# Two transformer-like layers on one core: part of the sum over phi(K) moves from TensorE to GpSimd and VectorE, with new instruction orders

## The chip, the core and the metric

One NeuronCore of a Trainium2 chip runs the whole program in one launch. The metric is the device time of one execution in microseconds (us), as the median of several runs. The engines are TensorE (PE in the profile, its weight loads PEld), VectorE (DVE), ScalarE (ACT), GpSimd (POOL) and SyncE (SP), which only issues transfers here.

## The reference

Input x has 2048 rows (tokens) of 512 values, in bf16. Two blocks A and B alternate twice (A, B, A, B), each added to x, with the layer norm in front applied twice in block B. Cut to what matters:

```python
def _A_ref(x, wqkv, wo):                       # 32 heads of 16
    q, k, v = heads(x @ wqkv)
    phi = lambda t: jnp.where(t > 0, t + 1, jnp.exp(t)) + 1e-6
    pq, pk = phi(q), phi(k)
    kv = jnp.einsum("bhsd,bhse->bhde", pk, v)
    z = jnp.einsum("bhsd->bhd", pk)            # the sum over all tokens
    num = jnp.einsum("bhqd,bhde->bhqe", pq, kv)
    den = jnp.einsum("bhqd,bhd->bhq", pq, z)[..., None] + 1e-6
    return (num / den) merged @ wo

def _B_ref(x, w1, b1, w2, b2):                 # 512 -> 1792 -> 512
    y = _layernorm(x)
    return gelu(y @ w1 + b1) @ w2 + b2

x = x + _A_ref(_layernorm(x), wqkv, wo)
x = x + _B_ref(_layernorm(x), w1, b1, w2, b2)
# and both once more
```

The change is about z in the first block A.

## The kernel before

The 2048 tokens are 16 tiles of 128, in 4 chunks of 4 tiles. "Layer one" is the first A and B (index 0 in names), "layer two" the second (index 1). The program builds a graph of some 1550 operations and plays them in an order that is written out by hand for each engine (`ORDER`), with fixed buffer places (`PLACES`) and, for steps that several engines can do, a fixed engine (`WAY`). Each engine works strictly through its own list; an operation whose input is not there holds up all that stand behind it. Names carry layer, chunk or tile, and part. SyncE issues the transfers, among them the transposing DMAs, also in a written order.

The steps, by the names used below (tile t, chunk c, layer L, part k):

- Norm of a tile: `statsA` and `aggrA` (L775, L777, VectorE), `vepsA` (L782) and `powA` (L784, GpSimd), then `normA` on VectorE (L803) or, with `nmrA` before it (L795, GpSimd), on ScalarE (L798). The norms of block B have the same names with B. `TA` and `TB` are the transposing DMAs of the result (L812, SyncE); the first tiles are transposed on TensorE instead (`PTC`, `PTA`, L825).
- `K L_t` (L879) and `Q L_c_k` (L896, L909): projections, each 4 matmuls of 128x512. phi is `exp` and `relu` on ScalarE (L847, L858), `min` (L860, L851) on VectorE, and `phik` or `phiq` (L864 as a sum, on VectorE or GpSimd; L853 as a maximum that reads PSUM, on VectorE). phi(K) of a tile lies in one of 10 buffers `pkb`.
- `G L_t_0` (L984 in layer one, L1013 in layer two): the products of normed x and phi(K), 4 matmuls a tile in layer one.
- z: `Z L_c` (L970) multiplies the four phi(K) tiles of a chunk by a column of ones, 16 matmuls with one column each, and `zs L_c` (L941, L944, VectorE) adds the four columns to `zs`. Layer one does so for all four chunks. Layer two does it for the last chunk only: the first three are added up in fp32 in `zacc` by `za` (L958, VectorE or GpSimd); then `zhi` (L923) and `zlo` (L926) split the sum into two bf16 parts and `ZH` (L933, L934), 8 matmuls with one column, gives z, which `zsh` takes over.
- From zs, `zb` (L1040) and `dz` (L1045) are made on VectorE. zb is the weight of `D 0_0_k` (L1100); dz gives `ZR` (L1048) and a row of z (L997). `KV`, `kvm` and `M` (L1034, L1053, L1057) fold wv, the G sums and wo into one weight `gtb`; its copies to SBUF are `cpg`, `cpz`, `cpm` (L997, L1000).
- The denominators of chunk 0: `D`, then `ln` and `rec` on ScalarE (L1102, L1104) and `pr` (L1108). Of the others, token by token: `pz` (L1077), `red` (L1080), `den`, `rec` (L1083, L1085), `pr` (L1089), and a transposing DMA `TP` (L1093).
- `WO` (L1123) and `RA` (L1128) close block A. Block B: `W1 L_c_f_h` with the chunk c (L1153; halves of 256 columns in chunk 0, h being the half), `gelu` (L1158), `b2` (L1139: x plus b2, VectorE or GpSimd), `W2 L_t_0` and `W2 L_t_7` (L1190, 7 matmuls each) and `RB` (L1196, L1200). `OD` stores the result. In names such as `W10_1_13_0` the first digit after W1 is the layer; `W20_0_7` is the second half of W2 of tile 0 in layer one.
- `warm` (L749) are matmuls on constants at the start. `wv`, `wo`, `w1`, `w2` are weight loads that GpSimd issues, `b1z` clears a buffer for `b1`, which SyncE loads and transposes (`Tb1`).

The order of TensorE around the change, layer one (parts left out):

```
... PTA0_2 K0_1 PTA0_3 K0_2 K0_3 G0_0_0 G0_1_0 Q0_0_2 Q0_0_1 Q0_0_0 K0_5 G0_2_0 K0_4 Z0_0 G0_3_0 ...
... K0_12 Z0_1 K0_15 K0_10 K0_8 K0_9 K0_11 G0_7_0 Q0_1_1 Z0_3 Q0_0_3 Z0_2 G0_8_0 G0_9_0 D0_0_2 ...
```

Of the kernel before, what the change touches and what calls it, by code (L numbers as in the profile page):

```python
# [1359 lines left out]
```

## Time and profile before

| | us |
|---|---|
| median of 3 runs | 323.65 (322.83 to 324.69) |
| the profiled execution | 323.1 |
| its span, first to last instruction | 321.9 |
| TensorE busy | 318.0 |
| VectorE busy | 218.1 |
| ScalarE busy | 189.3 |
| GpSimd busy | 145.5 |

The granted TensorE clock is 1.00 throughout. A line such as L958 is a line of this kernel's source. Several operations of one kind share a line, so a group of a line mixes layers; single instructions are found by their start in the span. A matmul's duration in the profile includes its way through the array (0.38 us for 128x512), while the chain that ended last gives the time from one to the next (0.86 us for four). "Waits" list how long an engine stood idle before an instruction, and which instruction ended the wait.

### The profile page before, as it was taken

How to read it: one execution, taken by the hardware profiler on the slowest of the kernel's cores; microseconds unless marked ns; L12 is line 12 of the kernel's file. 1: busy time of each engine (PE TensorE's matmuls, PEld its weight loads, DVE VectorE, ACT ScalarE, POOL GpSimd, SP SyncE). 2: the span in 40 equal slices, each digit the busy share in tenths (PEclk: the TensorE clock that was granted, in tenths of full speed). 3: DMA queues.
4: the chain of work that ended last, by engine and by line, in shares of the span. 5: the costliest groups of instructions: out<-in, count | busy, mean ns of one | idle time of the engine just before them, and what ended most of it. 6: DMA issues, size and time to landing. Idle time of an engine off the chain costs nothing.

```text
span 321.9 us, 4748 instructions
## 1 busy us (share of the span) xinstructions
PE 318.0 (99%) x1703; PEld 157.4 (49%) x1703; DVE 218.1 (68%) x529; ACT 189.3 (59%) x324; POOL 145.5 (45%) x216
## 2 busy tenths in 40 slices
PE   8999999999999999999999999999999999999997
PEld 3444554666444444444444444558544444444444
DVE  5998789999786774028848899999889881101103
ACT  5898656797730636667962367979634442663320
POOL 6573978688655355101822415887454163000000
DMA  7844793142121412111010200122232322201002
GB/s 257 200 81 85 241 348 85 35 82 36 33 49 34 82 33 51 34 33 32 18 40 10 51 16 0 35 51 52 50 62 54 98 65 67 49 0 35 16 33 65
DMA packets 52355, 21.68 MB, mean 67 GB/s; under 512 B 47532, under 2 KB 50860, under 8 KB 52332
## 3 DMA queue, kind: packets, MB, share of 16 engines
q1 hardware_dynamic: 50844, 16.37, 22.4%
q0 software_dynamic: 1056, 4.72, 4.3%
q10 hardware_dynamic: 432, 0.30, 0.3%
q8 instruction: 13, 0.21, 0.3%
q14 instruction: 10, 0.08, 0.1%
HBM read 8.00 MB, written 2.10 MB: 31 GB/s over the span
## 4 chain that ended last, share of the span: by engine, by line
PE 97%; DMA 2%; DVE 0%; issue 0%
PE ps L1153 30%; PE ps L1190 29%; PE ps L1123 9%; PE ps L879 8%; PE ps L896 6%; PE ps L984 4%; PE ps L1013 4%; DMA t<-in_A_x_dram 2%; PE ps L909 2%; PE ps L1176 1%; PE ps L970 1%; PE ps L1034 1%; PE ps L1057 1%; PE ps L1100 1%; DVE stats L775 0%; PE ps L1048 0%
## 5 line engine op out<-in xcount | busy, mean ns | idle before, releaser
L1158 ACT ACTIVATE gT<-ps,b1c 128x512 bf16<-128x512 f32 (+1 forms) x140 | 77.0, 601 | 68.7 <-PE ps L1153 68.1
L1153 PE MATMUL ps<-t,w 128*128 128x512 bf16 (+1 forms) x560 | 102.5, 336 | 0.0
L1190 PE MATMUL ps<-w,gT 128*128 128x512 bf16 x434 | 98.6, 379 | 0.0
L1153 PEld LDWEIGHTS ps<-t,w 128*128 128x128 bf16 x560 | 54.8, 98 | 43.7 <-ACT gT L1158 0.2
L1190 PEld LDWEIGHTS ps<-w,gT 128*128 128x128 bf16 x434 | 42.5, 98 | 50.4
L784 POOL TENSOR_TENSOR rstd<-veps,neghalf 128x1 f32<-128x1 f32 x64 | 39.0, 625 | 41.1 <-DVE veps L782 38.9
L847 ACT ACTIVATE eb<-ps 128x512 bf16<-128x512 f32 x62 | 35.4, 606 | 19.3 <-PE ps L896 7.3
L1200 DVE TENSOR_TENSOR yb<-ps,xsb 128x512 bf16<-128x512 f32 x15 | 10.2, 688 | 41.4 <-PE ps L1190 41.4
L775 DVE BATCH_NORM_STATS2 stats<-xsb 128x6 f32<-128x512 f32 x48 | 32.0, 681 | 0.3
L1123 PE MATMUL ps<-gtb,t 128*128 128x512 bf16 x128 | 31.4, 379 | 0.0
L879 PE MATMUL ps<-wqkv,t 128*128 128x512 bf16 x128 | 30.9, 379 | 0.3 <-ACT t L835 0.3
L858 ACT ACTIVATE rb<-ps 128x512 bf16<-128x512 f32 x43 | 25.3, 607 | 5.8 <-PE ps L879 5.8
L798 ACT ACTIVATE yb<-xsb,nmr,rstd 128x512 bf16<-128x512 f32 x21 | 16.9, 814 | 15.1 <-POOL nmr L795 15.1
L896 PE MATMUL ps<-wqkv,t 128*128 128x512 bf16 x96 | 24.1, 379 | 0.0
L1089 POOL TENSOR_TENSOR t<-t,rr 128x512 bf16<-128x512 bf16 x18 | 19.3, 1072 | 9.0 <-DVE rr L1085 6.4
L782 POOL TENSOR_SCALAR veps<-mv 128x1 f32<-128x1 f32 x35 | 8.2, 236 | 32.7 <-DVE mv L777 31.3
L1196 DVE TENSOR_TENSOR xsb<-ps,xsb 128x512 f32<-128x512 f32 x16 | 10.8, 678 | 17.9 <-PE ps L1190 17.9
L1139 POOL TENSOR_TENSOR xsb<-xsb,b2b 128x512 f32<-128x512 f32 x17 | 21.4, 1267 | 3.0 <-DVE yb L803 2.9
L1077 POOL TENSOR_TENSOR lr<-t,zrow 128x512 f32<-128x512 bf16 x14 | 16.5, 1179 | 7.3 <-ACT zrow L997 4.5
L1123 PEld LDWEIGHTS ps<-gtb,t 128*128 128x128 bf16 x128 | 12.5, 98 | 14.5
L803 DVE TENSOR_SCALAR yb<-xsb,mv,rstd 128x512 bf16<-128x512 f32 x27 | 14.5, 542 | 7.3 <-POOL rstd L784 6.0
L879 PEld LDWEIGHTS ps<-wqkv,t 128*128 128x128 bf16 x128 | 12.1, 98 | 14.7 <-ACT t L835 0.9
(99 smaller groups left out, 363.7 us busy)
## 6 DMA issues: line engine op xcount, KB each, us to landing
w<-in_B_w_dram POOLq DMA_DIRECT2D x4, 896.0 KB, 9.1
out_dram<-yb SPq DMA_DIRECT2D x15, 128.0 KB, 2.0
t<-in_A_x_dram SPq DMA_DIRECT2D x3, 512.0 KB, 4.8
t<-yb SPq DMA_TRANSPOSE x62, 2.5
wqkv<-in_A_wqkv_dram SPq DMA_DIRECT2D x1, 512.0 KB, 5.9
wqkv<-in_A_wqkv_dram POOLq DMA_DIRECT2D x1, 512.0 KB, 4.7
wo<-in_A_wo_dram POOLq DMA_DIRECT2D x1, 512.0 KB, 5.3
t<-in_A_x_dram SPq DMA_DIRECT2D x1, 384.0 KB, 3.3
```

Source lines behind the costliest of these rows:

```text
L775: G.op("dve", lambda e: e.bn_stats(stats[:, s.slot, :], src()), 620, reads=src_keys, writes=[k + "s"], tiles=[s, *src_tiles], name=f"stats ...
L784: G.op("pool", lambda e: e.tensor_tensor(rstd[:, s.slot:s.slot + 1], veps[:, s.slot:s.slot + 1], neghalf[:], op=ALU.pow), 570, reads=[k + ...
L847: G.op("act", lambda e: e.activation(eb[:, et.slot, :], bank(bt), ACT.Exp, scale=by()), 478, reads=[src_key, *more_keys], writes=[f"e{tag} ...
L858: G.op("act", lambda e: e.activation(rb[:, rt.slot, :], bank(bt), ACT.Relu, scale=by()), 478, reads=[src_key, *more_keys], writes=[f"r{tag ...
L879: ins = e.matmul(bank(b), lhsT=yTa(yT)[:, dt, k * P:(k + 1) * P], rhs=wqkv[:, dt, D:2 * D], start=(i == 0 and n == 0), stop=(i == len(part ...
L896: ins = e.matmul(bank(b), lhsT=yTa(yT)[:, dt, k * P:(k + 1) * P], rhs=wqkv[:, dt, 0:D], start=(dt == 0), stop=(dt == DT - 1))
L1089: lambda e, d=d, tok=tok, heads=heads: e.tensor_tensor(heads(tok()), heads(tok()), rr[:, d.slot, :].unsqueeze(2).broadcast_to([P, H, DH]), ...
L1123: ins = e.matmul(bank(wb), lhsT=yTa(pq)[:, kt, k * P:(k + 1) * P], rhs=gtb[:, kt, :], start=(kt == 0), stop=(kt == DT - 1))
L1139: G.op("pool" if on_pool else "dve", lambda e: e.tensor_tensor(xsb[:, st, :], xsb[:, st, :], b2b[:], op=ALU.add), 1120 if on_pool else 600 ...
L1153: ins = e.matmul(bank(b, n), lhsT=w1[:, dt, ft * P:(ft + 1) * P], rhs=yTa(yT)[:, dt, k0 * P:k1 * P], start=(dt == 0), stop=(dt == DT - 1))
L1158: G.op("act", lambda e, ft=ft, b=b, k0=k0, k1=k1, n=n: e.activation(gT[:, g.slot, ft * 512 + k0 * P:ft * 512 + k1 * P], bank(b, n), ACT.Ge ...
L1190: ins = e.matmul(bank(b), lhsT=gT[:, g.slot, ft * 512 + k * P:ft * 512 + (k + 1) * P], rhs=w2[:, ft, :], start=(ft == 0), stop=(ft == FT - 1))
```

## The change

In layer one, phi(K) of chunks 0 and 1 (8 tiles, 7 additions) is summed in fp32 in `zacc`: zaA1 and zaA3 to zaA7 on GpSimd, zaA2 on VectorE. Z0_0, Z0_1, zs0_0 and zs0_1 go; zhiA and zloA (VectorE), ZHA (TensorE, 8 matmuls with one column) and zshA (VectorE) come. The code for it was in `attn_z` already, and an entry of `WAY` selects it:

```diff
+        "zaA2": "dve", "zc0": "0 1",
```

The orders of all engines and the buffer places are chosen anew. Parts of TensorE's, VectorE's and GpSimd's:

```diff
 TensorE
-K0_5 G0_2_0 K0_4 Z0_0 G0_3_0 ... K0_12 Z0_1 K0_15 K0_10 K0_8 K0_9 K0_11 G0_7_0 Q0_1_1 Z0_3 Q0_0_3 Z0_2 G0_8_0 G0_9_0 D0_0_2
+Q0_1_0 K0_4 G0_2_0 K0_5 G0_3_0 ... K0_14 K0_10 K0_8 K0_11 K0_9 G0_7_0 Q0_0_3 Z0_3 G0_8_0 Z0_2 Q0_1_1 ZHA G0_9_0 D0_0_2
-W20_1_0 W10_0_10_0 W20_0_0 W10_0_9_1 ... W10_0_13_1 W10_0_5_1 W10_1_3_0 W10_1_9_0 W10_1_8_0
+W20_1_0 W20_0_0 W20_0_7 W10_0_4_1 W10_0_12_1 W10_0_5_1 W10_0_13_1 W20_1_7 W10_0_2_1 WO0_9_0 W10_0_7_1 W10_0_9_1 W10_0_8_1 W10_0_6_1 W10_0_0_1 W10_0_10_1 W10_1_13_0
 VectorE
-normA0_2 statsA0_5 normA0_3
+normA0_2 normA0_1 statsA0_4 normA0_3
-phik0_9 phik0_11 zs0_2 zs0_3 zb0 minq0_0_3 minq0_1_1 dz0
+mink0_10 zhiA phik0_10 mink0_9 mink0_11 phik0_9 phik0_11 zloA zs0_2 zs0_3 zshA zb0 dz0
-normB0_5 normB0_4 pz0_2_0
+pr0_2_1 normB0_5 RB0_0 minq0_3_0 red0_2_3 b20_1 statsA1_0 normB0_4
-cpm1_0 rec1_1_0 phiq1_1_3 rec1_1_1 RA1_0
+cpm1_0 pr1_0_2 pr1_1_0 rec1_1_1 phiq1_1_3 RA1_0
 GpSimd
-nmrA0_15 b1z nmrA0_8 powA0_12 vepsA0_10 powA0_10 vepsA0_11 powA0_11 nmrA0_10 vepsA0_9 powA0_9 nmrA0_11 phik0_14 eps6 wv wo phik0_8 w1_0
+nmrA0_15 zaA3 powA0_12 zaA4 vepsA0_10 powA0_10 nmrA0_10 vepsA0_8 zaA5 powA0_8 nmrA0_8 vepsA0_9 vepsA0_11 powA0_11 nmrA0_11 powA0_9 zaA6 zaA7 phik0_14 phik0_8 b1z wv wo w1_0
```

Other steps change engine in `WAY`: from GpSimd to VectorE 14 `b2` adds, 8 `pr`, 4 `pz`, 2 `za` and 12 of the small `veps`; from VectorE to GpSimd 2 `b2`, 3 `pr`, 3 `pz`, 1 `za` and 9 `veps`. The warm-up matmuls at the start keep their number and sizes; five of the 256 wide stand ahead of the first transpose instead of three. TensorE's order from `W11_3_11_0` on, late in layer two, is nearly the same. The code also gains a list of the order of chunks (`CHUNKS`, here 0 to 3 as before) and a way of treating half a chunk (`by_half`), which no entry of `WAY` uses.

More of the change, by code (lines that the diff above doesn't have):

```diff
@@ L887, in attn_q, with fn @@
         def attn_q(L, c, yT, pq):
-            if by_token(L, c):
-                for k in range(4):
+            half = by_half(L, c)
+            own = pq
+            if half:
+                own = tokq[(L, c)] = Tile(T4, f"pqt{L}_{c}")
+            n = 2 * P if half else 4 * P
+            if not by_token(L, c):
+                for kt in range(DT):
+                    b = Tile(psum, f"q{L}_{c}_{kt}" + "c" * half, "q")
+                    def fn(e, kt=kt, b=b):
+                        for dt in range(DT):
+                            ins = e.matmul(bank(b, n), lhsT=wqkv[:, dt, kt * P:(kt + 1) * P], rhs=yTa(yT)[:, dt, 0:n],
+                                           start=(dt == 0), stop=(dt == DT - 1))
+                        return ins
+                    G.op("pe", fn, 4 * MM if n == D else 4 * (n / 2.4 + 2.5), reads=[f"yT{L}_{4 * c + k}" for k in range(n // P)] + ["wq"], writes=[f"q{L}_{c}_{kt}" + "c" * half],
+                         tiles=[b, yT], name=f"Q{L}_{c}_{kt}" + "c" * half, lat=MM_DRAIN, n=4)
+                    phi(b, f"q{L}_{c}_{kt}" + "c" * half, lambda kt=kt: yTa(pq)[:, kt, 0:n], f"pq{L}_{c}_{kt}" + "c" * half, [pq], f"q{L}_{c}_{kt}" + "c" * half, n=n)
+            for k in range(4):
+                if by_token(L, c, k):
                     b = Tile(psum, f"q{L}_{c}_{k}", "q")
@@ L900, in attn_q, with attn_z @@
                          tiles=[b, yT], name=f"Q{L}_{c}_{k}", lat=MM_DRAIN, n=4)
[L901 removed]
+                    phi(b, f"q{L}_{c}_{k}", lambda k=k: t4[:, own.slot, k * D:(k + 1) * D], f"pq{L}_{c}_{k}", [own],
                         f"q{L}_{c}_{k}")
[L903 to L914 removed]
         zfirst = {}
[L918 to L920 removed]
+        def attn_z(L, c, pks, order):
+            by_sum = [int(v) for v in (eng("zc0") or "").split()] if L == 0 else order[:NC - 1]
+            others = [v for v in order if v not in by_sum]
             def fold(add):
@@ L973, in attn_z, with attn_g_held @@
             G.op("pe", fn, 400, reads=[f"pk{L}_{4 * c + k}" for k in range(4)] + ["onesm"], writes=[f"zc{L}_{c}"], tiles=[b, *pks], name=f"Z{L}_{c}", lat=MM_DRAIN, n=16)
-            total(b, f"zc{L}_{c}", f"zs{L}_{c}", bool(L) or c != min(v for v in range(NC) if v not in by_sum))
-            if L == 0 and by_sum and c == max(v for v in range(NC) if v not in by_sum):
+            total(b, f"zc{L}_{c}", f"zs{L}_{c}", bool(L) or c != others[0])
+            if L == 0 and by_sum and c == others[-1]:
                 fold(True)
-        def attn_g_held(L, st, k, y, ykey, pk, gb):
-            parts = [(dc,) for dc in range(DT)] if st == ST - 1 else [tuple(range(DT))]
+        def attn_g_held(L, st, k, y, ykey, pk, gb, first, last):
+            parts = [(dc,) for dc in range(DT)] if last else [tuple(range(DT))]
             for part in parts:
@@ L1004, in attn_g_out, with attn_g_chunk @@
                 copy(gtb[:, dc, :], gb, f"g{L}_{dc}", ("gt", dc), dc % 2, f"g{L}_{dc}", off=dc)
-        def attn_g_chunk(L, c, ys, ykeys, pks):
+        def attn_g_chunk(L, c, ys, ykeys, pks, first, last):
             for dc in range(DT):
@@ L1042, in attn_kv @@
                  reads=["zs", "bdmask"], writes=["zb"], name=f"zb{L}", lat=40, fast=True)
-            if any(by_token(L, c) for c in range(NC)):
+            if any(by_token(L, c, 3) for c in range(NC)):
                 zr = Tile(psum, f"zr{L}", "t")
@@ new lines, in attn_den @@
+            half = by_half(L, c)
+            src = tokq[(L, c)] if half else pq
+            pt = pq if half or not by_token(L, c) else Tile(T4, f"pt{L}_{c}")
+            n = 2 * P if half else 4 * P
+            if not by_token(L, c):
+                for kt in range(DT):
+                    tag = f"{L}_{c}_{kt}" + "c" * half
+                    b = Tile(psum, f"d{tag}", "n")
+                    r = Tile(LR, f"lr{tag}")
+                    key = f"pq{L}_{c}_{kt}" + "c" * half
+                    G.op("pe", lambda e, kt=kt, b=b: e.matmul(bank(b, n), lhsT=zb[:, kt * P:(kt + 1) * P], rhs=yTa(pq)[:, kt, 0:n], start=True, stop=True),
+                         MM if n == D else n / 2.4 + 2.5, reads=[key, "zb"], writes=[f"d{tag}"], tiles=[b, pq], name=f"D{tag}", lat=MM_DRAIN)
+                    G.op("act", lambda e, b=b, r=r: e.activation(lr[:, r.slot, 0:n], bank(b, n), ACT.Ln, bias=eps6[:]), 575 if n == D else 362,
+                         reads=[f"d{tag}", "eps6"], writes=[f"l{tag}"], tiles=[b, r], name=f"ln{tag}", lat=90, table="exp")
+                    G.op("act", lambda e, r=r: e.activation(lr[:, r.slot, 0:n], lr[:, r.slot, 0:n], ACT.Exp, scale=-1.0), 536 if n == D else 323,
+                         reads=[f"l{tag}"], writes=[f"l{tag}"], tiles=[r], name=f"rec{tag}", lat=110, table="exp")
@@ new lines, in attn_den, with attn_out @@
+                     1150 if on_pool else 600, reads=[f"rr{tag}", f"pq{tag}"], writes=[f"pq{tag}"], tiles=[d, src],
+                     name=f"pr{tag}", lat=60, fast=not on_pool)
+                dma("sp", lambda e, k=k, tok=tok: e.dma_start_transpose(yTa(pt)[:, :, k * P:(k + 1) * P], tok()), [f"pt{tag}"],
+                    tiles=[src, pt], reads=[f"pq{tag}"], name=f"TP{tag}", sem=("pT", src, k), transpose=True)
+            return pt
+        def attn_out(L, c, k, pq, base, base_keys, base_tiles, first):
@@ L1116, in attn_out @@
             st = 4 * c + k
             wb = Tile(psum, f"wo{L}_{st}", "w")
-            parts = [(kt,) for kt in range(DT)] if st == 0 else [tuple(range(DT))]
+            parts = [(kt,) for kt in range(DT)] if first else [tuple(range(DT))]
             for part in parts:
@@ L1141, in mlp_front, with mlp_up @@
                  fast=not on_pool)
-        def mlp_up(L, c, yT, g):
-            parts = [(0, 2), (2, 4)] if c == 0 else [(0, 4)]
+        def mlp_up(L, c, yT, g, first):
+            parts = [(0, 2), (2, 4)] if first else [(0, 4)]
             for hf, (k0, k1) in enumerate(parts):
@@ L1206, in build_kernel @@
         gb = Tile(psum, "g4", "g4", 4)
-        pq1, trs = [], []
-        for c in range(NC):
+        pq1, trs = {}, []
+        orders = cf["CHUNKS"]
+        for c in orders[0]:
             yT = Tile(T4, f"yT0_{c}")
             pq = Tile(T4, f"pq0_{c}")
-            pq1.append(pq)
+            pq1[c] = pq
             pks = []
@@ L1252, in build_kernel @@
         for L in range(2):
-            nxt = []
-            for c in range(NC):
+            nxt = {}
+            chunks = orders[1 + L]
+            for c in chunks:
                 yT = Tile(T4, f"yBT{L}_{c}")
```

141 lines of the change are left out of this document (58 added, 83 removed), and 483 rows, old and new, of tables (ORDER, PLACES, WAY).

## The prediction

> **What bounds the kernel now.** I read the page's first two parts, then the chain that ended last, the waits of TensorE, and the engines by stage; last, single instructions of VectorE and GpSimd. From the page:
>
> ```profile
> PE 318.0 (99%) x1703; PEld 157.4 (49%) x1703; DVE 218.1 (68%) x529; ACT 189.3 (59%) x324; POOL 145.5 (45%) x216
> ...
> PE   8999999999999999999999999999999999999997
> ...
> DVE  5998789999786774028848899999889881101103
> ...
> PE 97%; DMA 2%; DVE 0%; issue 0%
> ```
>
> TensorE is busy in every slice and is 97% of the chain. VectorE is full in slices 2 to 10 and 21 to 28. TensorE's own waits:
>
> ```profile
> PE ps L749 <- PEq L1345: 0.8, 1, 0.8
> PE ps L825 <- DVE yb L803: 0.5, 1, 0.5
> PE ps L879 <- ACT t L835: 0.3, 1, 0.3
> PE ps L825 <- DVE yb L789: 0.2, 1, 0.2
> ```
>
> All four lie before 9.6 us; the last ends at 9.16, where the fourth transpose starts (PTA0_3). It follows normA0_3, queued on VectorE behind the first statistics of chunk 1, whose load lands at 8.07. From 9.16 on TensorE stands in no wait, so after it only TensorE work that goes away can shorten the run, and any new wait lengthens it. The profiled execution took 323.1 us (span 321.9 and 1.2 around it), 0.55 below the median of the runs, 323.65. The sum is made on 323.1 and moved up by 0.55.
>
> **What goes and comes on TensorE.** The chain shows a Z group of 16 matmuls (L970) and the ZH group of 8 (L933, L934), with the work behind each:
>
> ```profile
> 18.19 0.38 PE ps L970 x16
> 18.57 0.89 PE ps L984 x4
> ...
> 189.40 0.00 PE ps L933
> ...
> 189.58 1.75 PE ps L1013 x8
> ```
>
> A Z group costs 0.38, and the four matmuls behind it 0.89 instead of 0.86 (28.09, same view): 0.41. Z0_0 and Z0_1 go: 0.82. ZHA comes at the price of ZH: 189.58 - 189.40 = 0.18, and 1.75 behind it instead of 1.73 (11.28): 0.20. Net -0.62. All other matmuls stay in number and shape.
>
> **The start** stays. Warm-up pieces change places, but normA0_3 again stands behind one statistics instruction (statsA0_4 for statsA0_5) that needs the same load, and PTA0_3 stands ahead of K0_2 as before. Bounds: -0.2 to +0.2, taken 0.
>
> **The new wait.** ZHA is followed by one G group (0.86) and then D0_0_2, whose weights are zb. Between them VectorE does zshA and zb0; before, D0_0_2 had two G groups behind Z0_2. Rows: VectorE starts its sum 0.04 after the last Z matmul leaves the chain (37.04 to 37.08), L941 takes 0.16, zb begins 0.04 later (37.44 to 37.48), L1040 takes 0.69, a weight load 0.10: 1.03, against 0.86 of cover. That is +0.17, taken +0.2; behind D0_0_2 stands all of TensorE's queue. Bounds: 0 (TensorE late there anyway) and +0.7 (one more 0.69 instruction late ahead of zshA).
>
> **VectorE in layer one.** Added: zaA2 0.69 (L958), zhiA 0.42 (L923), zloA 0.68 (L926), zshA 0.16; removed: two sums of 0.15 and 0.16. Net 1.64. From the busy times by stage:
>
> ```profile
> core 0: us, PE busy (x) PEld busy (x) DVE busy (x) ACT busy (x) POOL busy (x), PEclk, DMA share, GB/s
> 9.60:20.00 10.40, 10.40 (x64) 4.83 (x63) 9.86 (x33) 9.88 (x19) 6.67 (x17) 1.00 0.64 125
> 20.00:30.00 10.00, 10.00 (x62) 4.67 (x61) 8.89 (x28) 9.11 (x17) 5.26 (x14) 1.00 0.46 92
> 30.00:40.00 10.00, 10.00 (x77) 4.98 (x75) 8.22 (x20) 7.04 (x14) 7.95 (x10) 1.00 0.65 196
> ```
>
> Each row gives the stretch, its length and the engines' busy times. VectorE's are 9.86 + 8.89 + 8.22 = 26.97 of 30.4: it has 30.4 - 26.97 = 3.43 us free, so 1.64 fits. But the six adds on GpSimd (L958, 1.16 each, 7.0 in all) also lengthen VectorE instructions beside them:
>
> ```profile
> 31.42 1.15 POOL L864 TENSOR_TENSOR pkb<-eb,rb 128x512 bf16<-128x512 bf16 x1 [4.94 <-DVE eb L860]
> 32.18 0.54 DVE L851 TENSOR_SCALAR eb<-eb 128x512 bf16<-128x512 bf16 x1
> 35.48 0.83 DVE L864 TENSOR_TENSOR pkb<-eb,rb 128x512 bf16<-128x512 bf16 x1
> 153.05 1.68 POOL L1139 TENSOR_TENSOR xsb<-xsb,b2b 128x512 f32<-128x512 f32 x1
> 153.63 1.25 DVE L860 TENSOR_SCALAR eb<-eb 128x512 bf16<-128x512 bf16 x1
> ```
>
> L851 is 0.29 in the median and took 0.54 until that GpSimd instruction ended; L864 (0.42) took 0.83 beside the one at 34.88; in layer two L860 (0.285) took 1.25. So a meeting costs 0.25 and 0.41 in this stage and 0.96 at worst. Six at the mean of the near rows, 0.33, are 2.0: 1.64 + 2.0 = 3.6, just the 3.43 that are free. Taken: no stall; bounds 0 and 6 x 0.96 + 1.64 - 3.43 = +4.0.
>
> [...] The rows above agree that VectorE gets on when GpSimd ends, and that statistics and PSUM sources (L775, L853) keep their 0.69 beside it. [...]
>
> **GpSimd in layer one.** Behind zaA3, zaA4 and zaA5 stand the small steps of the last norms (powA0_12, 10, 8, 11, 9); the transposes TA0_x and then K0_x wait for them. The worst is powA0_9. In the trace its like ends at 26.1; three adds are 3.5 more, less about 1.9 of GpSimd's idle time between 14 and 25 us: 27.7, or 29.6 if none of it serves. With L803 0.41 and a transposing DMA 2.5 (median from issue to landing) K0_9 can start at 30.6 to 32.5. Before, the last K group started at 32.8; less 0.82 it starts at 31.98. Taken 0, bound +0.5. zaA6 and zaA7 end before phik0_14's old start, 31.42, plus at most 1. b1z, wv, wo, w1 and w2 are issued behind phik0_8, up to 2 us later; b1 and Tb1 on SyncE wait for b1z, and TP0_1_3 stands behind them, but its data come only at 48. wv (issue to landing 4.7) is then there by about 41, KV0_0 is at 46.8. Nothing.
>
> **The moved steps behind layer one.** b2 adds: 14 go from GpSimd to VectorE and 2 back; pr: 8 and 3; pz: 4 and 3. In 60 to 120 us that is about 7 x 0.68 + 3 x 0.68 + 0.69 = 7.5 us more on VectorE, with 60 - 48.7 = 11.3 free, and some 12 us less of GpSimd work that meets it. Two places lose cover. (a) normB0_4 now stands behind RB0_0, which waits for W20_0_7. From there VectorE needs 0.68 + 0.29 + 0.67 + 0.68 + 0.68 + 0.54 = 3.54, the transpose 2.5: 6.1. TensorE has 16 x 0.109 + 1.51 + 0.44 + 0.86 + 24 x 0.109 = 7.2 until W10_1_13_0. Cover 1.1; one meeting of 0.96 uses it up, the longest transpose (4.6) would cost 1.0. (b) W11_0_2_0 at 215.28 needs TB1_1, which lands near 214.8 (normB1_1 ends 212.12). pr1_0_2 and pr1_1_0 go in front of RA1_0 on VectorE (1.36) against 0.42 of wait there and steps moved away from between: 0 to +0.5. Both taken 0. The last 40 us have VectorE 10% to 20% busy and TensorE's order of before; nothing.
>
> **Sum.** -0.62 + 0.2 = -0.42: 322.7 for a profiled execution, 323.2 for the median. About 0.5% (1.6 us) is what a measurement of this kernel can tell from no change, so this is no change.
>
> **Rivals.** (1) GpSimd shuts VectorE out: it decides if the six adds take over 1.8 us from VectorE (3.43 - 1.64), 0.3 each; phi(K), the last K groups and zb come late and TensorE waits between 25 and 40 us. At 0.96 each the price is +4.0: 323.65 - 0.42 + 4.0 = 327.2; at 0.75 each, 6 x 0.75 + 1.64 - 3.43 = +2.7: 325.9. For it: VectorE is at 95% from 9.6 to 20 us. Against: near rows of 0.25 and 0.41, and many instructions there (statistics, PSUM sources) do not lengthen. Chance of over 0.5% slower: 0.11.
> (2) The thin cover of (a) and (b) and of K0_9 fails together with zb: +1.0 + 0.5 + 0.5 + 0.5 more: 325.7. Each alone stays within 0.5%. Chance of a sum that large 0.05.
> (3) More is won: TensorE has no wait after 9.16, so the most is -0.62 and the 0.7 between K0_1's end and 9.16 if chunk 1 lands sooner: 322.3. That is still no change; beyond 0.5% only by the scatter of the runs (322.83 to 324.69): 0.06.
> (4) The change does not do what it says, because the two Z groups were hidden: speaks against it that both are pieces of the chain. 323.65, inside the forecast.
>
> **Numbers.** Forecast (no change, with the small stalls and rivals 3 and 4 inside 0.5%) 0.78; its own range 322.1 to 325.2. Slower 0.16, faster 0.06. The range reaches to 325.9 for the milder form of rival 1.
>
> **What would show it.** Right: PE busy time near 317.4, 5 groups of Z down to 3 and two ZH; D0_0_2 with a VectorE wait (zb, L1040) of about 0.2; no wait elsewhere after 9.2 us; L958 on GpSimd 1.2 to 1.4; VectorE over 95% busy from 9.6 to 35. Wrong: TensorE waits on pkb (phi(K)) or on transposes before 40 us, or on t ahead of W10_1_13_0 or W11_0_2_0, or a start later than 9.4.

## The result: 0.85% slower, and the profile after

The changed kernel takes 326.25 us (median of 9 runs, 324.88 to 328.11) beside 322.98 for the kernel before on the same chip: a ratio of 1.0085, 95% interval 1.0059 to 1.0112. Run a second time it takes 326.28 (6 runs, 326.11 to 327.18) beside 323.04: 1.0098, 1.0081 to 1.0115. The forecast was no change at 323.2, with a range of 322.1 to 325.9. The result lies above that range, and beyond the 0.5% that the prediction took as the line between "no change" and "slower".

The page of the changed kernel (its profiled execution: 327.56 us, span 326.3), with the rows that were shown of before:

```profile
PE 318.1 (97%) x1649; PEld 156.8 (48%) x1679; DVE 228.6 (70%) x553; ACT 192.5 (59%) x326; POOL 133.3 (41%) x200
...
PE   6999999998999999999999999999999999999997
...
DVE  5898989999787879005579899999798884100103
...
PEclk9899999999999999999999999999999999999999
...
PE 78%; DVE 13%; POOL 3%; ACT 3%; DMA 1%; issue 1%; SPq 0%; DVEq 0%
```

TensorE's busy time has not gone down (318.0 to 318.1, in a second profile of the same kernel 318.8, where about 317.4 was expected; the first lacks some 30 matmul records). Its first slice is at 6 instead of 8 and the tenth at 8; VectorE's digits in slices 2 to 10 are those of before but for two; and the chain that ended last is no longer TensorE alone: 13% of it is VectorE and 3% GpSimd. So something now stands between TensorE and its work. Its own waits, in us in total, times, longest:

```profile
PE ps L886 <- ACT t L842: 1.6, 1, 1.6
...
PE ps L1170 <- ACT gT L1175: 0.8, 1, 0.8
PE ps L886 <- ACT eb L854: 0.6, 1, 0.6
PE ps L886 <- DVE pkb L860: 0.3, 1, 0.3
PE ps L886 <- DMA t<-yb: 0.3, 1, 0.3
```

The lines have moved: K is L886 now, the copy of the first transposes L842, exp L854, phi's maximum L860, W1 L1170, gelu L1175. The first wait, ahead of the first K, was 0.3 (the start). Four are new: W1 for gelu, and K for exp, for phi(K) and for a transposing DMA. The second profile (326.11 us, span 324.9) shows which of them are the change's and which were chance:

```profile
PE ps L1170 <- ACT gT L1175: 1.3, 1, 1.3
...
PE ps L886 <- ACT eb L854: 0.6, 1, 0.6
PE ps L886 <- ACT t L842: 0.6, 1, 0.6
PE ps L886 <- DVE pkb L860: 0.3, 1, 0.3
```

The start's wait went from 1.6 to 0.6; those for gelu, exp and phi(K) came back. I cut every run into the same stretches, by the starts of single TensorE instructions: up to PTA0_3 (the start), PTA0_3 to D0_0_2 (stretch A, all of the moved sum), the first WO of layer one to the first KV of layer two (stretch B), and from that KV to TensorE's last matmul, 117.78 in before and changed alike. Between A and B lie 12.3 us, alike too.

| kernel | start | A | B | profiled run | median |
|---|---|---|---|---|---|
| before | 9.16 | 29.47 | 151.18 | 323.1 | 323.65, beside the changed one 322.98 |
| changed | 10.78 | 31.29 | 152.19 | 327.56 | 326.25 |
| changed, second time | 8.68 | 31.48 | 152.66 | 326.11 | 326.28 |

The differences add up: -0.48 + 2.01 + 1.48 = 3.01 for the second profile, which is 326.11 - 323.1. For the first, 1.62 + 1.82 + 1.01 = 4.45 against 4.46; it is 1.3 above its own median because of its start, which is dealt with at the end. There are two places to explain: A, expected at 29.47 - 0.42 = 29.05, and B, expected to stay. In A the busy times by stage are, in the columns of the prediction's table, from the second profile:

```profile
core 0: us, PE busy (x) PEld busy (x) DVE busy (x) ACT busy (x) POOL busy (x), PEclk, DMA share, GB/s
9.60:20.00 10.40, 10.40 (x49) 4.50 (x48) 10.13 (x30) 9.70 (x19) 8.96 (x20) 1.00 0.72 133
20.00:30.00 10.00, 9.57 (x43) 3.66 (x40) 8.93 (x26) 8.18 (x16) 9.04 (x16) 1.00 0.33 66
30.00:40.00 10.00, 9.23 (x76) 4.21 (x76) 8.83 (x21) 6.16 (x12) 6.08 (x7) 1.00 0.22 37
60.00:80.00 20.00, 18.73 (x132) 12.53 (x130) 19.52 (x50) 14.91 (x28) 12.70 (x17) 1.00 0.26 54
```

TensorE has 0.43 and 0.77 us idle in 20 to 40 us and 1.27 in 60 to 80, all of it 0 before. In A alone 2.6 are lost, 2.01 and the 0.62 of work that is gone; a matmul of 128x512 is recorded as 0.38 long, while four take 0.86 from start to start, so short gaps don't show as idle. From start to start they do, and by that TensorE loses 0.77 ahead of one K (30.42, for exp) and 0.43 ahead of the next (31.73, for phi(K)), 0.24 to 0.31 each at three more (an exp, a relu, a transposing DMA), 0.26 at D0_0_2 (zb) and 0.3 in two small ones. In B nearly all is one gap: W1 at 77.37 comes 1.43 late. VectorE was busy 26.97 of 30.4 us before and is now 10.13 + 8.93 + 8.83 = 27.89: it still has 2.5 us free while TensorE stands. The prediction had looked for a full VectorE; that isn't what one sees here.

### The profile page after: what moved, and what is told of

Same layout as the page of the kernel before. It is cut to its first block, busy times and chain, and to the rows that moved or that the text cites. A ratio compares the mean times of both kernels' runs of the same rounds, so it can differ in the third digit from the quotient of the medians.

```text
span 326.3 us, 4676 instructions
## 1 busy us (share of the span) xinstructions
PE 318.1 (97%) x1649; PEld 156.8 (48%) x1679; DVE 228.6 (70%) x553; ACT 192.5 (59%) x326; POOL 133.3 (41%) x200
## 4 chain that ended last, share of the span: by engine, by line
PE 78%; DVE 13%; POOL 3%; ACT 3%; DMA 1%; issue 1%; SPq 0%; DVEq 0%
PE ps L1170 26%; PE ps L1207 24%; PE ps L1140 6%; PE ps L886 6%; PE ps L919 4%; PE ps L1025 4%; DVE stats L782 3%; PE ps L996 2%; DVE xsb L1145 2%; POOL rstd L791 1%; PE ps L907 1%; DMA t<-in_A_x_dram 1%; DVE yb L810 1%; POOL veps L789 1%; PE ps L1193 1%
## 5 line engine op out<-in xcount | busy, mean ns | idle before, releaser
L1175 ACT ACTIVATE gT<-ps,b1c 128x512 bf16<-128x512 f32 (+1 forms) x140 | 77.4, 601 | 62.9 <-PE ps L1170 62.6
L1170 PE MATMUL ps<-t,w 128*128 128x512 bf16 (+1 forms) x555 | 102.1, 336 | 1.1 <-ACT gT L1175 0.8
L1207 PE MATMUL ps<-w,gT 128*128 128x512 bf16 x425 | 97.6, 379 | 0.5
L1170 PEld LDWEIGHTS ps<-t,w 128*128 128x128 bf16 x560 | 54.7, 98 | 44.6 <-ACT gT L1175 1.5
L791 POOL TENSOR_TENSOR rstd<-veps,neghalf 128x1 f32<-128x1 f32 x64 | 40.1, 631 | 36.6 <-DVE veps L789 32.1
L854 ACT ACTIVATE eb<-ps 128x512 bf16<-128x512 f32 x62 | 35.2, 602 | 18.8 <-PE ps L919 12.1
L886 PE MATMUL ps<-wqkv,t 128*128 128x512 bf16 x128 | 33.6, 390 | 2.8 <-ACT t L842 1.6
L1140 PE MATMUL ps<-gtb,t 128*128 128x512 bf16 x124 | 30.5, 379 | 0.3
L789 POOL TENSOR_SCALAR veps<-mv 128x1 f32<-128x1 f32 x32 | 11.1, 346 | 44.9 <-DVE mv L784 43.0
L805 ACT ACTIVATE yb<-xsb,nmr,rstd 128x512 bf16<-128x512 f32 x21 | 16.8, 807 | 16.4 <-POOL nmr L802 11.9
L1123 POOL TENSOR_TENSOR t<-t,rr 128x512 bf16<-128x512 bf16 x15 | 16.6, 1109 | 19.1 <-DVE rr L1119 15.4
L919 PE MATMUL ps<-wqkv,t 128*128 128x512 bf16 x92 | 23.3, 379 | 0.2
L1156 DVE TENSOR_TENSOR xsb<-xsb,b2b 128x512 f32<-128x512 f32 x27 | 18.6, 706 | 5.0 <-ACT yb L805 5.0
L886 PEld LDWEIGHTS ps<-wqkv,t 128*128 128x128 bf16 x128 | 12.0, 99 | 19.5 <-ACT t L842 2.2
L1111 POOL TENSOR_TENSOR lr<-t,zrow 128x512 f32<-128x512 bf16 x13 | 15.2, 1168 | 7.4 <-ACT zrow L1009 3.9
```

Of the source, the lines that this page charges most:

```text
L791: G.op("pool", lambda e: e.tensor_tensor(rstd[:, s.slot:s.slot + 1], veps[:, s.slot:s.slot + 1], neghalf[:], op=ALU.pow), 570, reads=[k + ...
L854: G.op("act", lambda e: e.activation(eb[:, et.slot, 0:n], bank(bt, n), ACT.Exp, scale=by()), 478 if n == D else 265, reads=[src_key, *more ...
L886: ins = e.matmul(bank(b), lhsT=yTa(yT)[:, dt, k * P:(k + 1) * P], rhs=wqkv[:, dt, D:2 * D], start=(i == 0 and n == 0), stop=(i == len(part ...
L919: ins = e.matmul(bank(b), lhsT=yTa(yT)[:, dt, k * P:(k + 1) * P], rhs=wqkv[:, dt, 0:D], start=(dt == 0), stop=(dt == DT - 1))
L1140: ins = e.matmul(bank(wb), lhsT=yTa(pq)[:, kt, k * P:(k + 1) * P], rhs=gtb[:, kt, :], start=(kt == 0), stop=(kt == DT - 1))
L1156: G.op("pool" if on_pool else "dve", lambda e: e.tensor_tensor(xsb[:, st, :], xsb[:, st, :], b2b[:], op=ALU.add), 1120 if on_pool else 600 ...
```

## Experiments

Each run stands beside runs of the kernel before on the same chip. A and B are the stretches above.

**Which part of the order carries the loss.** First the sum itself is taken back, on otherwise the changed kernel:

```diff
 TensorE
-G0_3_0 K0_7 ... G0_6_0 K0_14 ... Q0_1_1 ZHA G0_9_0
+G0_3_0 Z0_0 K0_7 ... G0_6_0 Z0_1 K0_14 ... Q0_1_1 G0_9_0
 VectorE, GpSimd: zaA1 to zaA7, zhiA, zloA, zshA out; zs0_0, zs0_1 back
```

> The changed kernel with the sum in fp32 undone in layer one: Z0_0, Z0_1, zs0_0, zs0_1 back (Z0_0 behind G0_3_0, Z0_1 behind G0_6_0), zaA1 to zaA7, zhiA, zloA, ZHA and zshA gone; every other order, place and engine as in the changed kernel. Theory ADDS (the additions on GpSimd and VectorE hold up the norms and phi(K), which costs about 2.5 us of TensorE's 4.4 in the profile): TensorE gets 0.6 more work but loses the stalls between 13 and 35 us, about 326.3 + 0.6 - 2.5 = 324.4. Theory ORDERS (the new orders alone cost it, the start among them): the stalls stay, 326.3 + 0.6 = 326.9. Theory START (all from the late start and the throttled clock): 326.9 as well, and TensorE's start of K0_2 at 11.0 again.

Measured: 325.53 beside 323.5 (6 runs), ratio 1.006 (1.0037 to 1.0082). A is 30.26 instead of 31.48, B 151.41 instead of 152.66. So with no sum at all, the new order of layer one still costs 0.8 us in A, of which 0.5 is one wait of this kernel's own (K for the bank that zs0_0 reads). B went nearly back, although not one instruction behind 50 us was touched; that needed its own explanation. Another 0.39 lies between A and the first WO. The profiled run, 324.49, was the lowest of the six, 1.0 below their median; whether B was longer in the others isn't known.

Then the changed orders up to K0_2 are replaced by those of before:

```diff
 TensorE
-warm0 warm7 warm3 warm4 warm5 warm1 PTC0 warm8 warm2 K0_0a K0_0b warm6 K0_0c PTC1 K0_0d PTA0_2
+warm0 warm8 warm2 warm6 PTC0 warm1 warm7 warm5 warm4 warm3 K0_0a K0_0b PTC1 K0_0c K0_0d PTA0_2
 VectorE
-normA0_1 statsA0_4 normA0_3
+statsA0_5 normA0_3 aggrA0_5 normA0_1 statsA0_4
```

> The changed kernel with the orders of all engines up to the start of K0_2 as in the kernel before (five of the small warm-up pieces behind PTC0 again, statsA0_5 ahead of normA0_3, and so on), all behind it as changed. Theory START: K0_2 starts near 9.5 instead of 11.0 and the clock stays at 1.00 in the first 10 us, so 326.3 - 1.6 = 324.7. Theory CHANCE (the load of the first chunk landed 0.95 us late by chance in the one profiled execution, and the runs do not have it): 326.3, no different. Theory ADDS: the lead of 1.6 us is lost again between 13 and 35 us because VectorE sets the pace there: 326.3, with more TensorE idle time in that stretch.

326.37, ratio 1.0085 (1.0065 to 1.0104): nothing is gained. A is 31.52. The start isn't it. The next two join the halves of the two orders at the first WO (51 us):

```diff
 first: changed up to the first WO, before behind it    second: the other way round
-M0_3 Q0_2_2 WO0_0_0 ... W20_1_0 W20_0_0 W20_0_7        (TensorE of the changed kernel)
+M0_3 Q0_2_2 WO0_0_0 ... W20_1_0 W10_0_10_0 W20_0_0     (first)
+Q0_2_2 M0_3 Q0_2_3 WO0_0_0 ... W20_1_0 W20_0_0 W20_0_7 (second)
```

> The changed kernel up to the first WO (some 51 us: the new start, the additions, the new orders of layer one's block A), and from there the orders, engines and places of the kernel before. Theory ADDS and theory START both put the loss before 51 us: at the first W1 TensorE is 3.4 us late in the profile, and 323.0 + 3.4 = 326.4. If the wait for normB0_6 and the gelu at 78 us is a loss of its own, about 1.0, then 325.3.

> The converse: the kernel before up to the first WO (its start, Z0_0 and Z0_1 on TensorE), and from there the orders, engines and places of the changed kernel (b2, pr and pz on VectorE, normB0_4 behind RB0_0, and so on). Theories ADDS and START: nothing is lost behind 51 us, 323.0. Theory LATER (VectorE is overloaded from 55 to 79 us by the steps moved to it, so normB0_6 and gelu come late): 324.0 or more, with a TensorE wait for gT near 75 to 79 us.

The first took 326.3 (1.0075, 1.0056 to 1.0094), the second 324.4 (12 runs; 1.0029, 1.0012 to 1.0046). A goes with the first half: 31.48 against 29.61. B doesn't split so cleanly: 152.11 in the first, where WO waits 0.7 for VectorE at the joint, and 152.62 in the second, where W1 waits 1.1 for a transposing DMA. (The first also waits 0.7 for a transposing DMA at 259 us, in layer two and behind B; that belongs to neither stretch.) In the second, one instruction is there that I found in the changed kernel too: a `veps` on GpSimd of 2.12 us. It ends in no wait for gelu here, because TensorE is already late by the DMA; so this run doesn't test what that instruction costs. I come back to it.

**Stretch A: two ways for GpSimd's adds to reach TensorE.** What the second profile of the changed kernel shows between 23 and 32 us (start, duration, instruction, idle before it and what ended that; the last line is TensorE's group that waited):

```profile
23.38 0.81 ACT L805 ACTIVATE yb<-t,nmr,rstd 128x512 bf16<-128x512 bf16 x1 [1.07 <-POOL nmr L802]
...
23.70 1.15 POOL L970 TENSOR_TENSOR zacc<-zacc,pkb 128x512 f32<-128x512 f32 x1
23.90 1.23 DVE L871 TENSOR_TENSOR t<-eb,rb 128x512 bf16<-128x512 bf16 x1
...
28.09 0.81 ACT L805 ACTIVATE yb<-t,nmr,rstd 128x512 bf16<-128x512 bf16 x1 [0.74 <-POOL nmr L802]
...
28.54 2.38 POOL L970 TENSOR_TENSOR zacc<-zacc,pkb 128x512 f32<-128x512 f32 x2
...
29.76 1.31 DVE L810 TENSOR_SCALAR yb<-t,mv,rstd 128x512 bf16<-128x512 bf16 x1
...
30.42 1.04 PE L886 MATMUL ps<-wqkv,t 128*128 128x512 bf16 x4 [0.60 <-ACT eb L854]
```

Read it as two stories. *Lock*: L871 (phi as a sum of two SBUF tiles) at 23.90 takes 1.23 instead of 0.42 and ends, 25.13, 0.28 behind the add on GpSimd that began before it (zaA5, 23.70); the norm L810 at 29.76 takes 1.31 instead of 0.41 beside zaA7. *Queue*: the norms on ScalarE, L805, stand 1.07 and 0.74 us idle for `nmr`, a 128x1 step on GpSimd that comes behind an add in GpSimd's list. ScalarE takes the exps behind these norms only after them: behind the norm of 28.09 the next exp starts at 28.81, and the one that K needs at 29.77. So the PSUM bank that this exp frees comes late, and K waits 0.60 for it (30.42). The wait of 0.27 for phi(K) at 31.73 belongs to the lock: the maximum that ends it (L860) starts at 30.99, right behind the lengthened norm. In the kernel before, two instructions of these kinds take

```profile
23.52 0.42 DVE L864 TENSOR_TENSOR t<-eb,rb 128x512 bf16<-128x512 bf16 x1
...
26.26 0.41 DVE L803 TENSOR_SCALAR yb<-t,mv,rstd 128x512 bf16<-128x512 bf16 x1
```

To tell the two stories apart: zaA4 and zaA5 go behind the small steps (no queue, lock left); the adds become fills that read nothing (queue left, and the rows show whether the lock is); and the six are left out (as in the last diff of this section).

```diff
 GpSimd, adds behind the norms
-nmrA0_15 zaA3 powA0_12 zaA4 vepsA0_10 ... vepsA0_8 zaA5 powA0_8 ... powA0_9 zaA6 zaA7
+nmrA0_15 zaA3 powA0_12 vepsA0_10 ... vepsA0_8 powA0_8 ... powA0_9 zaA4 zaA5 zaA6 zaA7
 GpSimd, fills for zaA3 to zaA7
-e.tensor_tensor(zacc, zacc, pkb, op=add)      # 128x512, 1.15 us
+e.memset(gacc, 0.0)                           # 128x1300 fp32, 1.18 us
```

> The changed kernel with four of GpSimd's additions (zaA4 to zaA7) moved behind powA0_9, the last small step of the norms on GpSimd; nothing else moved. TensorE's stretch from the fourth transposes (PTA0_3) to D0_0_2 takes 31.3 to 31.5 us in the changed kernel and 29.5 in the kernel before, with 0.6 less work of its own in the changed one, so some 2.5 us are stalls. Theory QUEUE (the norms' small steps stand behind the additions in GpSimd's list, so normA0_8 and normA0_11 on ScalarE, the exp behind them and the PSUM banks come late): the stretch falls to about 29.6 and the time to 326.3 - 1.8 = 324.5. Theory LOCK (the additions stretch VectorE's instructions beside them, wherever they stand): the additions meet VectorE a few us later, stretch and time stay, 326.3.

> The changed kernel with zaA3 to zaA7 on GpSimd replaced, in the same places and behind the same waits, by a fill of 1300 fp32 columns with zeros in a buffer that layer one does not use (an instruction that writes only and takes about as long as an addition); the sums of these five tiles are left out. Theory QUEUE: GpSimd's list is as slow as before, the stretch from PTA0_3 to D0_0_2 stays at 31.3 to 31.5 and the time at 326.3. Theory LOCK: if fills leave VectorE alone, its phi instructions (L871) and normA0_9 are at 0.42 again instead of 1.0 to 1.3, the stretch falls to about 29.5 and the time to 324.5; if fills stretch VectorE's instructions as well, the rows show that and the run tells nothing.

> The changed kernel with the six additions on GpSimd left out (zaA2, zhiA, zloA, ZHA and zshA stay, so the sum lacks six tiles); all orders otherwise as changed. Both theories QUEUE and LOCK: the stretch from PTA0_3 to D0_0_2 falls to 28.9 to 29.2 (29.5 less 0.6 of TensorE work, plus up to 0.3 of the new wait for zb) and the time to 326.3 - 2.4 = 323.9. Theory ORDERS (the new order of layer one loses time by itself): the stretch stays above 30.5, the time at 325.5 or more.

| kernel | A | median beside | ratio (95%) |
|---|---|---|---|
| adds behind the norms | 31.20 | 326.02 / 323.15 | 1.0082 (1.0050 to 1.0114) |
| fills for adds | 31.35 | 325.86 / 323.15 | 1.0079 (1.0057 to 1.0102) |
| six adds left out | 29.89 | 323.88 / 323.15 | 1.0023 (1.0003 to 1.0044) |

The six adds are the cost: without them A is 1.6 shorter than with them (31.48 - 29.89), and with zaA2, zhiA and zloA still on VectorE. But taking away one of the two stories takes away almost nothing. With the queue gone, K no longer waits for exp, but the adds met VectorE's min three times (L858 at 1.12, 0.64, 0.72 instead of 0.29) and the norm again (L810 at 1.31), and K waited 0.5 for phi(K) and 0.4 for the phi(Q) of L860, whose bank it needs. With fills, the queue's wait of 0.61 was there as before, and part of the lock was there too, on the norms (two at 0.83 and 1.34):

```profile
24.36 1.18 POOL L970 MEMSET gacc<- 128x1300 f32 x1
24.57 0.40 DVE L871 TENSOR_TENSOR t<-eb,rb 128x512 bf16<-128x512 bf16 x1
...
29.21 2.44 POOL L970 MEMSET gacc<- 128x1300 f32 x2
...
30.45 1.34 DVE L810 TENSOR_SCALAR yb<-t,mv,rstd 128x512 bf16<-128x512 bf16 x1
31.11 1.04 PE L886 MATMUL ps<-wqkv,t 128*128 128x512 bf16 x4 [0.61 <-ACT eb L854]
```

Beside a fill at the same place as zaA5, L871 takes 0.40 instead of 1.23, but the norm L810, with one SBUF tile in and one out, takes 1.34 again. So in these rows a fill lengthens the norm and not the sum of two SBUF tiles, where the adds lengthened both (1.31 against 0.41, 1.23 against 0.42); why isn't shown.

Since neither half alone was the answer, I put each onto the kernel before, where nothing else differs: four spare adds whose result nobody needs, behind the last norm step (lock alone); and three fills ahead of norm steps (queue, as near to alone as a fill allows).

```diff
 GpSimd of the kernel before, spare adds
-powA0_9 nmrA0_11 phik0_14
+powA0_9 nmrA0_11 add add add add phik0_14
 GpSimd of the kernel before, fills
-nmrA0_15 b1z ... powA0_12 vepsA0_10 ... vepsA0_11 powA0_11
+nmrA0_15 fill b1z ... powA0_12 fill vepsA0_10 ... vepsA0_11 fill powA0_11
```

> The kernel before with four spare additions (fp32 plus bf16, 128x512, into a buffer that layer one does not use) on GpSimd behind nmrA0_11, in the 4.9 us in which GpSimd is idle before phik0_14; nothing waits for them and TensorE's work is that of before. LOCK by itself: VectorE's min, phi and norm instructions between 26 and 32 us are stretched by 0.25 to 1.0 each, the stretch from PTA0_3 to D0_0_2 grows from 29.5 to 30.0 to 30.9, the time from 323.2 to 323.7 to 324.6. If only GpSimd's list counts (QUEUE): 323.2, as phik0_14 is hardly later.

> The kernel before with three fills of 1300 fp32 columns (1.18 us each, into a buffer that layer one does not use) on GpSimd in the places that zaA3, zaA4 and zaA5 have in the changed kernel: behind nmrA0_15, behind powA0_12 and behind vepsA0_11. QUEUE by itself: the norms of tiles 8 to 12 come up to 3.5 us later, less the idle time GpSimd has there (about 1.9), the transposes and K0_8 to K0_15 with them; the stretch grows from 29.5 to 30.0 to 31.0, the time from 323.2 to 323.7 to 324.7. If the norms have cover enough: 323.2.

Spare adds: 324.98 beside 323.04, 1.0058 (1.0041 to 1.0076); A 31.02, so +1.55. Fills: 324.75, 1.0054 (1.0034 to 1.0073); A 31.16, +1.69. B stays 151.17 to 151.18 in both. The spare adds show the lock without any dependence:

```profile
26.11 1.12 POOL L1224 TENSOR_TENSOR gacc<-onesm 128x512 f32<-128x512 bf16 x1
26.26 1.26 DVE L871 TENSOR_TENSOR t<-eb,rb 128x512 bf16<-128x512 bf16 x1
27.31 3.82 POOL L1224 TENSOR_TENSOR gacc<-gacc,onesm 128x512 f32<-128x512 f32 x3
27.44 1.24 DVE L858 TENSOR_SCALAR eb<-eb 128x512 bf16<-128x512 bf16 x1
...
29.47 2.76 PE L886 MATMUL ps<-wqkv,t 128*128 128x512 bf16 x12 [0.38 <-DVE t L860]
30.11 1.30 DVE L871 TENSOR_TENSOR t<-eb,rb 128x512 bf16<-128x512 bf16 x1
```

Three VectorE instructions of 0.42, 0.29 and 0.42 take 1.26, 1.24 and 1.30: 2.7 us lost for four adds, and K waits 0.38 and, at 32.40 and 33.87, 0.17 and 0.43 for L860, the maximum that comes late behind them. The fills weren't a pure queue:

```profile
23.36 1.25 DVE L810 TENSOR_SCALAR yb<-t,mv,rstd 128x512 bf16<-128x512 bf16 x1
...
25.32 1.04 PE L919 MATMUL ps<-wqkv,t 128*128 128x512 bf16 x4 [0.80 <-DVE t L860]
```

Beside them L858 took 1.05, L810 1.25 and L867 1.15 instead of 0.29, 0.41 and 0.28, 2.5 us in sum, and TensorE's two long waits, 0.80 and 0.23, were both for VectorE's L860. So the lock alone is shown to suffice for 1.55, and the 1.69 of the fills may be the lock as well. The queue's own share isn't separated; for it speaks the wait for exp in the changed kernel, which is gone when the queue is and stays at 0.61 where L871 is free.

Is the placing of the change at fault then, or the sum? The same sum in before's orders, with the adds put behind the small steps of the norms and ZHA ahead of Z0_2:

```diff
 GpSimd of the kernel before
-nmrA0_7 vepsA0_13 ... nmrA0_11 phik0_14 eps6
+nmrA0_7 zaA1 vepsA0_13 ... nmrA0_11 zaA3 zaA4 zaA5 zaA6 phik0_14 zaA7 eps6
 VectorE
-phik0_2 statsA0_12 ... phik0_9 phik0_11 zs0_2 zs0_3 zb0
+phik0_2 zaA2 statsA0_12 ... phik0_9 zhiA phik0_11 zloA zs0_2 zs0_3 zshA zb0
```

> The kernel before, all its orders kept, with the sum in fp32 alone put in: Z0_0, Z0_1, zs0_0, zs0_1 go; zaA1 behind nmrA0_7, zaA2 on VectorE behind phik0_2, zaA3 to zaA6 behind nmrA0_11 (the last step of the norms on GpSimd), zaA7 behind phik0_14; zhiA and zloA behind phik0_9 and phik0_11 on VectorE, ZHA ahead of Z0_2, zshA behind zs0_3. Theory ORDERS (the new orders are what costs): TensorE has 0.6 less to do and the time is 322.6. Theory LOCK (the additions meet VectorE wherever they stand): four additions in a row stretch VectorE's min, phi and norm, the stretch from PTA0_3 to D0_0_2 grows from 29.5 to 30.5 or more, the time to 324.2 or more.

330.02 beside 323.04, 1.0213 (1.0188 to 1.0239); A is 34.85. Its TensorE waits:

```profile
PE ps L886 <- DVE t L860: 1.8, 1, 1.8
PE ps L945 <- DVE eb L938: 1.6, 1, 1.6
```

L945 is ZHA: beside four adds in a row VectorE falls behind (L871 1.38 and L858 1.24), and TensorE stands 1.8 for a bank that phi(Q) frees; zhiA then starts late and itself takes 1.50, and TensorE stands 1.6 for the sum. (0.7 of this profile is a wait for a transposing DMA at 262 us, far behind the sum.) The orders of the changed kernel are better for this sum than the old ones with the adds placed so, by 3.7 us; it is the sum that costs.

**Stretch B: one step of 128x1.** The second profile of the changed kernel:

```profile
68.28 0.54 DVE L810 TENSOR_SCALAR yb<-xsb,mv,rstd 128x512 bf16<-128x512 f32 x1
...
68.50 2.12 POOL L789 TENSOR_SCALAR veps<-mv 128x1 f32<-128x1 f32 x1
...
69.28 0.69 DVE L1156 TENSOR_TENSOR xsb<-xsb,b2b 128x512 f32<-128x512 f32 x1
69.88 0.69 DVE L1111 TENSOR_TENSOR lr<-t,zrow 128x512 f32<-128x512 bf16 x1
70.48 0.68 DVE L1114 TENSOR_REDUCE rd<-lr 128x32 f32<-128x512 f32 x1
...
72.32 0.81 ACT L805 ACTIVATE yb<-xsb,nmr,rstd 128x512 bf16<-128x512 f32 x1 [1.97 <-POOL nmr L802]
...
73.15 1.28 ACT L1333 ACT_TABLE_LOAD   x1
...
77.37 0.61 PE L1170 MATMUL ps<-t,w 128*128 128x256 bf16 x4 [1.26 <-ACT gT L1175]
```

vepsB0_6, 128 values, starts on GpSimd 0.22 behind a norm on VectorE and takes 2.12 us: it ends 0.05 behind the last of VectorE's norm, phi, min, b2 and pz, which run back to back, when a reduce (L1114) has begun. powB0_6, nmrB0_6 and normB0_6 on ScalarE follow (idle 1.97 for nmr); behind that norm ScalarE loads its tables for two exps and back (73.15 and 75.54, 1.28 each), and W1 waits 1.26 for the gelu that comes after. In before this step stood on VectorE; it is one of the nine `veps` that went to GpSimd. In the kernel with the Z groups back, the same step at the same place in the same lists:

```profile
67.59 0.54 DVE L810 TENSOR_SCALAR yb<-xsb,mv,rstd 128x512 bf16<-128x512 f32 x1
...
67.81 0.38 POOL L789 TENSOR_SCALAR veps<-mv 128x1 f32<-128x1 f32 x1
68.05 0.42 DVE L871 TENSOR_TENSOR t<-eb,rb 128x512 bf16<-128x512 bf16 x1
```

It starts 0.22 behind the norm as well, and gets through in 0.38. It was 2.12 in five profiles with these orders (both of the changed kernel, those with before's start, with the adds behind the norms, and with before's first half) and 0.38 in three (Z groups back, fills, no adds), with nothing between. In the three, W1 doesn't wait for gelu and B is 151.2 to 151.4. None of the three has an add on GpSimd in layer one behind zaA1; of the five with 2.12 only the one with before's first half has none either. Whether the adds, 40 us earlier, have a part in that or it is chance, eight profiles don't tell. Moved to VectorE, behind aggrB0_6:

```diff
 GpSimd
-nmrB0_7 vepsB0_6 powB0_6
+nmrB0_7 powB0_6
 VectorE
-aggrB0_6 minq0_2_3
+aggrB0_6 vepsB0_6 minq0_2_3
```

> The changed kernel with one small instruction moved: vepsB0_6 from GpSimd to VectorE (behind aggrB0_6), where the kernel before has it. Theory SHUT OUT (the 128x1 instruction on GpSimd takes 2.13 us because VectorE runs three instructions with two SBUF inputs in a row beside it; nmrB0_6, normB0_6, two table loads and the gelu that TensorE waits for at 78 us come late): the wait of 0.8 to 1.3 us for gT goes, and the time falls to 326.3 - 1.1 = 325.2. Rival: the chain is late anyway because VectorE is full from 55 to 75 us; normB0_6 and the wait stay, 326.3.

325.0 beside 323.15, ratio 1.0071 (1.0044 to 1.0098): the median is 1.25 below the changed kernel's, though the intervals of the two ratios overlap; the better evidence is the profile, where B is 151.84. It doesn't go all the way since now the pair of powB behind it is caught (2.72 instead of 1.13), with W1's wait down to 0.32:

```profile
70.62 2.72 POOL L791 TENSOR_TENSOR rstd<-veps,neghalf 128x1 f32<-128x1 f32 x2 [0.17 <-DVE veps L789]
```

**Both causes out.** Last, the changed kernel without the six adds and with vepsB0_6 on VectorE:

```diff
 GpSimd
-powA0_5 zaA1 vepsA0_6 ... nmrA0_15 zaA3 powA0_12 zaA4 ... zaA5 powA0_8 ... powA0_9 zaA6 zaA7 phik0_14 ... vepsB0_6
+powA0_5 vepsA0_6 ... nmrA0_15 powA0_12 ... powA0_8 ... powA0_9 phik0_14 ...
 VectorE
-aggrB0_6 minq0_2_3
+aggrB0_6 vepsB0_6 minq0_2_3
```

> The changed kernel with both suspected causes taken out: the six additions on GpSimd left out (the sum lacks six tiles) and vepsB0_6 on VectorE. If the additions and the shut-out small instruction are the whole cause, the time is that of the kernel before, 323.2, to within 0.5, and the profile shows no wait for gT and a stretch from PTA0_3 to D0_0_2 of 29.9 again. If the orders hold a third cause behind 51 us, the time stays near that of the run without the additions, 323.9, or above. With both causes out, TensorE's 0.6 less work would give 322.6 at best; if that is reached, the orders cost nothing.

323.84 beside 323.19 (12 and 18 runs): 1.0015, interval 1.0000 to 1.0030. Its profiled execution took 323.19, A 29.80, B 151.21. So with the two causes out, 0.15% of the 0.85% is left, which can hardly be told from nothing. How much of that is the second edit's can't be read from it: without the adds alone the ratio was 1.0023, and there the small step took 0.38 and B was 151.18 anyway. TensorE's waits behind the warm-up are

```profile
...
PE ps L886 <- ACT t L842: 0.4, 2, 0.3
PE ps L886 <- DMA t<-yb: 0.3, 1, 0.3
```

The first line lies at the start, the second is a K at 21.86; the waits for gelu, exp and phi(K) are gone.

> The changed kernel once more, for a second profile beside these runs. If the late start of its first profile was chance (first chunk landed at 5.5 instead of 4.6, then 1.6 us without TensorE work and a clock of 0.87), PTA0_3 starts near 9.0 when the chunk lands by 4.7 and the clock is 1.00; the stretch to D0_0_2 is 31.2 to 31.5 again; the wait for gT near 77 us is there if vepsB0_6 takes 2.1 us and not if it takes 0.4. Time 326.3 in the median, as before. If the start belongs to the new order: PTA0_3 at 10.5 or later again.

That last run, the changed kernel once more, is the second profile used throughout: A and B came back within 0.2 and 0.5, the start didn't. No version with the sum came out below the kernel before.

## Why the prediction was wrong

- **TensorE's work, -0.62: right, and used up.** In the second profile ZHA takes 39.02 to 39.21, 0.19 for the 0.20 predicted, and two Z groups are gone. With both causes out, A should then be 29.47 - 0.62 = 28.85, and is 29.80; from start to start, 0.49 of these 0.95 is lost at a K that waits for a transposing DMA, 0.26 at D0_0_2 (zb) and 0.17 at a K that waits for ScalarE's copy of the fourth transposes. So the 0.62 is there, and small waits of the new order take it back.
- **The new wait for zb, +0.2: right.** zshA 39.21, zb0 39.41 for 0.70, D0_0_2 at 40.16. The four matmuls of G0_9_0 start at 39.04 and take 0.86 from start to start, to 39.90: 0.26 are lost.
- **VectorE in layer one, taken 0: the step that failed first.** "1.64 + 2.0 = 3.6, just the 3.43 that are free. Taken: no stall." The price of the meetings was about right: in the second profile three meetings lengthen VectorE by 0.58 + 0.81 + 0.90 = 2.3 (L871 beside zaA3 and zaA5, L810 beside zaA7), where 2.0 was taken. What was wrong is the comparison with free time. (By its own figures 3.6 was more than the 3.43, too, and of slices 2 to 10 and 21 to 28, called full, slice 21 shows a 4.) The 3.43 were an average over 30 us, while each lengthened instruction stands in the way of one phi(K) or one transpose with a time of its own; VectorE kept 2.5 us free and TensorE lost over 2. The four spare adds show that 2.7 us taken from an engine with 3.43 free cost TensorE 1.55.
- **GpSimd in layer one, taken 0, bound +0.5: failed too.** I followed powA0_9 to its transpose and to K0_9, which is the last to be needed. The adds also hold up nmrA0_10 (behind zaA4) and nmrA0_11 (behind zaA5), and these are waited for by ScalarE, with exps queued behind the norms. "Who waits for that" was asked for one consumer only; K's wait of 0.60 for exp comes from here, though its share of the 2.0 lost in A isn't separated from the lock's.
- **The moved steps, (a) and (b) at 0: both right, and beside the point.** Neither W10_1_13_0 nor W11_0_2_0 waited. But the sum of VectorE's load for 60 to 120 us went by b2, pr and pz; the nine `veps` that came to GpSimd were named in the diff and costed by no step. One of them is B's +1.0 to +1.5. In the second profile this missing term, 1.48, is over a third of the error: 3.01 found and -0.42 forecast are 3.43 apart.
- **The rivals.** Rival 1 had the right sign and place, and its condition was met: the adds took 2.3 us, over 1.8. Its range, 325.9 to 327.2, held the result, but by luck: with the measured 2.3 its own sum is 2.3 + 1.64 - 3.43 = +0.5, so 323.7. It used the same free time of 3.43, came to its range by 0.75 to 0.96 for each of six meetings, and has no place for B. In A the queue on GpSimd is a second route beside the lock, as far as the waits show. The chance of 0.11 was too low for a condition that my own 2.0 already fulfilled: the estimate stood above the point from which the rival decides, and I still called it "just fits". The price differed from add to add: three of the six lengthened next to nothing (beside zaA6 the min takes 0.42 instead of 0.29, beside zaA4 the norm its 0.41), and the other three cost 0.58 to 0.90, none of them the whole 1.15 of an add. Rivals 2 to 4 were not seen: the covers held, nothing more was won, and the sum is where the change says.
- **What was to show it wrong, did:** K waits on phi(K) before 40 us.

## What to carry to other kernels

Free time of an engine over a stretch is no room for work that lengthens its instructions (here 2.7 us out of 3.43 free cost 1.55): ask which of them has a consumer that is just in time, and count the lengthening there. When long instructions are put into the list of an engine that also does small steps, follow every small step behind them to its consumer, and to what is queued behind that consumer on its own engine. And cost every line of the diff: one 128x1 step that moved between engines came with a W1 1.43 us late here, more than the 0.62 that went from TensorE.
